# Block with adaLN, sliding-window attention and a gated MLP: w_q and later loads behind a wait for the modulation weights, a new instruction order

## The chip, the cores and the metric

The kernel runs on one core of one Trainium2 chip. The metric is device time in microseconds (us) of one execution; the number given for a kernel is the median over its timed runs. A profiled execution has its own time, and a span, which is the time from its first to its last instruction.

## What is computed

One block over a sequence of 2048 tokens of width 448 (bfloat16), cut from the reference:

```python
mod = (silu(c) @ w_mod).reshape(c.shape[0], 6, 1, -1)
sa, ca, ga, sb, cb, gb = (mod[:, i] for i in range(6))
h = layernorm(x) * (1 + ca) + sa
x = x + ga * A(h, wqkv, wo)
h = layernorm(x) * (1 + cb) + sb
x = x + gb * B(h, w_in, w_sp, b_sp, w_out)

def A(x, wqkv, wo):            # H = 16 heads of 28, window W = 256
    q, k, v = split(x @ wqkv)
    scores = q @ k.T * 28 ** -0.5
    mask = (i - j >= 0) & (i - j < W)
    return softmax(where(mask, scores, -1e9)) @ v @ wo

def B(x, w_in, w_sp, b_sp, w_out):
    z = gelu(x @ w_in)                       # 448 -> 1792
    z2 = layernorm(z[..., 896:])
    g = w_sp @ z2 + b_sp                     # mixing over the 2048 tokens
    return (z[..., :896] * g) @ w_out
```

The modulation (`mod`) is one vector of 6 x 448 numbers for all tokens. Its first two parts, sa and ca, are wanted before anything of the attention can be computed from x, since each normalized token is scaled and shifted by them.

## The kernel before

**Tiles.** The 2048 tokens are 16 tiles of 128; four tiles make a block `tb` (0 to 3). x stays in SBUF as `x_sb`. For each tile the kernel takes statistics on DVE (`bn_stats`, `bn_aggr`; function `stats`, L626 to L633), raises the variance to the power -1/2 on POOL (L633), normalizes into `xn` (`norm`, L644 on DVE or L651 on POOL) and transposes to `hT`, features on partitions. Block 0 is transposed on PE (L740) and modulated while it is copied out of PSUM (L748 to L751, on ACT or DVE). Blocks 1 to 3 are transposed by DMA, issued by SP (`turn`, L467), and modulated in place (L729 to L732).

**Attention.** `hT` times `WQK` gives Q (L797 for block 0, L763 later) and K (L821); `hT` times `wv` gives V (L841). `WQK` is a copy of the loaded `wq_st` in which each head of 28 is padded to 32 columns; function `wqk` (L615, L616) makes it in eight copies, four for K (`t_wqkk`) and four for Q (`t_wqkq`), each on ACT, DVE or POOL. Scores (L906 to L967) go to PSUM, ACT takes the exponential (L912), DVE masks (L975, L996), PE multiplies with V (L1003), DVE divides (L1017, L1019), a DMA transpose and `wo_g` follow (L1029), and DVE adds x (L1033). The second layer norm, its DMA transpose and its modulation (L1052, L1054) prepare the MLP: z from L1123 and L1144, the mixing over tokens L1168, the last product L1187, the output L1197 and L1202.

**Modulation.** The row c is turned to a column by four tiny products (`t_cT`, L514), ACT takes SiLU of it (`t_sc`, L517; it needs a table load, and the exponential later needs another). Thirty-two products with `wmodA` (`t_mA`, four groups of eight, L544) give sa and ca, which DVE copies to `modT` (`t_modA`, L573, L574). The other four parts come later from `wmodB`. While PE would have nothing to do at the start it runs products on a tile of ones (`fillers`, function `warm`, L563): 30 long and 6 short ones, whose results nobody reads.

**Loads at the start.** SP and ACT issue them, each in its own order. c (`t_c`), x in pieces (`t_x0[0]`: tiles 0 and 1; `t_x0[1]`: tiles 2 and 3; `t_x[1]`: tiles 4 to 7; `t_x[2]`, `t_x[3]`: the rest), `wmodA` in four quarters of 196 KB (`t_wmA`; 0 and 2 on SP, 1 and 3 on ACT), the K and the Q columns of wqkv in two halves each (`t_wk`, `t_wq`; half 0 on SP, half 1 on ACT), the V columns (`t_wv`, SP), and `wmodB`, 1568 KB (`t_wmB`, SP).

**The order.** Every operation is an `Op` with a number in order of its making, the engines that could run it, and the operations that it depends on (`deps`). The text `PLAN` names for each operation its engine (p PE, a ACT, d DVE, t POOL, s SP), its number and, behind points, the PSUM bank or buffer that it takes: `p42.1` is operation 42 on PE with the second choice of bank. Each engine runs its words in the order of the text and never overtakes. `Sched.waits` turns dependencies between engines into semaphore waits in front of the waiting instruction. `after` and the priorities given beside the operations served the search that wrote the text, and put no instruction into the program; `deps` do.

Numbers that the change and the prediction use: 0 `t_c`; 1, 10 `t_x0`; 2 to 5 `t_wmA`; 6, 7 `t_wk`; 8, 9 `t_wq`; 11 `t_wv`; 12 to 14 `t_x[1:]`; 15 `t_wmB`; 34 to 36 the mask on POOL; 37 `t_cT`; 38 SiLU; 39, 40 clearing `QBD`, a block-diagonal copy of Q (40 waits for `t_x[1]`); 42 to 45 `t_mA`; 46 to 81 fillers; 82, 83 `t_modA`; 100 to 103 `t_wqkk`; 104 to 107 `t_wqkq`; 108 to 111 and 116 to 119 the statistics of tiles 0, 1 and of 2, 3; 112, 184 sums of variance and epsilon (`ve_all`); 114, 115, 122, 123 `xn` of tiles 0 to 3; 125, 126, 128, 129 the modulated transposes of tiles 0, 1 and 131, 132, 134, 135 of tiles 2, 3; 136 to 149 K and Q products and evictions of tiles 0, 1; 176 to 183 the statistics of tiles 4 to 7; 185 their power; 186 and 188 to 192 their `xn`; 193 to 196 their DMA transposes; 373 the first exponential.

Of the kernel before, what the change touches and what calls it, by code (L numbers as in the profile page):

```python
# [15 lines left out]
p65.0 p78.1 d82 d125 d128 t101 p139.1 t25 t102 p56.0 d126 p81.3 p76.1 p47.0 p80.3 p59.2 p53.1 p49.2 a105 t103  # L16
d129 p140 a141 a40 p148.5 p149 a150 d116 d118 d117 d119 d176 d180 d182 d178 d177 d183 d181 d179 t104 t107
p145.6 p146 a147 p136.1 p137 a138 s11 p151.5 p152 a153 p79.2 t120 t121 d123.0 d122.1 p130.7 p133.0 a134 d41
d131 t184 t185 d186.3 p68.0 p372.0 a373.2 p142.6 p143 a144 d132 d135 p154.7 p170.1 p171 p155 p378.0 s13 d241
d247 d245 s14 d308 d242 d156 d246 s15 s193 t187 t188.1 s194 p163.0 p164 t189 t190.2 s195 t191 t192.0 s196  # L20
a379.4 p397.0 t34 t35 d248 t36 d243 d382 d312 d306 d380 d309 d374 d376 p173.6 a172 p157.1 p158 p160.7 p174
a398.1 a165 p90.0 p91 d92 a399 p404.0 d402 d310 d244 d400 d169 p161 p93.0 t85 t84 a175 a159 p86.1 p87 d88 d89
p375.0 p377 p94 a405.3 a406 p425.0 p381 p383 a197 d199 t200 d198 p210.1 p211 t249 t250 t252 t253.2 t254 d95
p217.0 p218 s16 s19 a426.0.0 p433.0 d384 d385.1 p401.0 s386 a166 d407 p403 p408 a212 p204.1 p205 d311 d219
p201.0 p202 d409 s259 t255.1 d307 d313 t314 d167 d168 s260 d251.0 t256 s258 t257.3 s261 t315 t321 t319 t99 t98
t96 t97 a434.2 p453.0 d429 d203 d436 a206 p207.1 p208 p410 d411 d209 d430 d412.2 s413 d435 a162 p427.0 p220.0
p221 a454.1.1 p461.0 p229.1 p230 d457 a428 a222 p226.0 p227 d228 p431.0 p432 a462.6 p481.0 d463 a231 a482.4.2
s852 s17 s18 p437 p438 d439 d215 d440.1 s441 p223.0 p224 a225 p232.1 d458 d216 d213 d464 p489.0 a490.2 d492
p233 p235.0 p236 a237 p459.0 p455.0 p508.0 p414.0 p415 d416 t262 t264 t263 t265 a234 p387.1 p388 d389 d486
a456 p460 p465 p466 d467 d468.0 d485 t320.1 s325 t322.2 s469 s326 s21 a214 p483.0 p272.0 p273 a509.0.0 p536.0  # L30
p269.1 p270 d491 p487.0 a484 p510.0 p488 p493 a537.5.1 p516.0 d274 d316.0 s323 t317 t318.3 p494 d390 d391 t392
t393 d512 d513 d495 d496.1 s497 d394.1 t395 s324 t330 t327 t329 a271 a511 p266.1 p267 p538.0 p275.0 p276
a517.6 d519 d518 d417 p564.0 a268 p442.1 a277 p282.0 p443 p514.0 d444 d281 p515 p283 a565.4.2 d569 p544.0 d418
d445 t419 d278 p291.1 p520 p521 d522 d446 d540 d447 d541 a539 p292 a284 p288.0 p289 t448 t449 s396 t450.0 t328
t451 s20 s848 d523.1 s524 a545.2 p572.0 d546 d547 d568 a293 p294.1 p295 a290 p238.0 p239 p542.0 p543 p548
a573.0 d574 p592.0 p549 d550 d551.0 s552 s846 a240 p470.0 p471 p566.0 a296 p285.1 p286 d472 d279 a593.3.0
p600.0 p300.0 d575 d473 d596 d280 p570.0 p301 d302 a567 p571 p576 a601.2 p619.0 d602 p577 d597 d578 d579.1
s580 a287 p525.1 p337.0 p338 d474 p526 d527 a620.4.1 p627.0 d624 d623 d603 p594.0 a339 p553.0 p554 d555 p340.1
p598.0 p341 a628.5 p647.0 d475 d630 a595 p599 p604 d556 p605 d606 d607.0 s608 s452 t476 t477 t478.2 t420 t421
t422.1 d557 t423 t479 s480 s424 t558 t559 t560 a342 p498.1 p499 p621.0 d500 p297.0 p298 a648.6.2 p675.0 d629  # L40
d651 a622 p649.0 p625.0 p331.1 p332 a299 p334.0 p626 a676.3.0 p655.0 d501 d502 t503 d333 d652 d528 d679 p631
p632 p335 d633 d336 d344 a650 p347.1 p677.0 p348 a656.4 d657 p683.0 a678 a349 p609.0 p610 d611 d658 d680
d634.2 s635 a684.5 p359.1 p360 a361 p350.0 p351 a352 d612 d343 d613 d346 d345 p703.0 a704.2.1 d707 t504 d505.0
d686 t561.1 t562 t822 t614 t615 p353.1 p354 a355 p303.0 p304 a305 p653.0 p711.0 p654 p659 p660 d661 d662.1
s663 p356.1 p705.0 p581.0 p582 a712.1 p730.0 d685 d583 d713 d708 p681.0 p682 p687 p688 d689 d690.2 d714 a706
a731.0.2 d735 d734 p732.0 a733 t821 s563 s691 s853 s847 t506 s507 d529 t530 p357 d358 p738.0 a739.5 p365.0
p709.0 p710 p715 p366 a367 p716 d717 d584 d718.1 s719 t531 t532 t533.1 d585 t586 t824 t823 t534 t587 t588
t589.2 d740 d741 p758.0 a759.1.1 d763 p760.0 p362.0 p363 a364 a761 p664.1 p665 d666 d762 p736.0 p766.0 a767.3
p737 p742 p743 d744 d745.2 s746 d667 d768 p368.0 p369 p636.1 p786.0 d769 p637 d638 a370 p764.0 p692.0 p693
d694 p765 p770 s535 s371 a787.4.2 d790 p794.0 a795.2 p771 d772 d773.0 s774 d668 d669 t670 t671 t672.0 d590  # L50
s591 d791 t673 s674 d796 d639 d797 d640 d695 d696 t697 t698 t699 p788.0 a789 p720.1 p721 d722 d723 d616.1 d617
p747.0 p792.0 p870.0 p871.1 p872 p793 p798 p799 a874 s866 p873 s618 d641 t642 d876 t700.0 t701 s702 p748 d749
# [12 lines left out]
a1050 a1051 a1053 s844 s843 s838 s865 s851 s839 s841 s869 s849 s864 s863 s859 s854 s867 s862 s837 s868 s856
d1009 d995 d1010 d1002 d1003 d970 d1004 d898 d952 d959 t820 t1011 t1012 d1013 t976 d977 t1005 d1006 p1109.0
p1115.1 d1116.1 p1118.5 p1076.3 p1112.7 p1124.4 d1119.0 t1120 p1070.5 t1117 d1113.1 t1114 t817 p1106.6 d1107.1
t1108 p1121.2 d1122.1 t1123 d1125.1 t1126 p1079.7 d1080.0 t1081 p1085.6 d1071.1 t1072 d1077.1 t1078 s857 s860
s855 s861 s858 p1142.1 p1139.7 d1086.0 p1172.6 t1087 d1143.0 d1110.1 t1111 t1144 t819 t816 p1127.3 d1140.1
t1141 p1184.0 d1185.1 t1186 p1187.4 d1188.0 t1189 p1082.2 d1083.1 t1084 p1175.1 p1181.7 d1128.0 d1176.0  # L70
p1157.0 p1130.4 d1131.2 t1177 d1158.0 p1136.5 d1137.1 p1148.1 d1149.1 t1159 t1150 d1182.1 d1173.0 t1183
p1178.3 p1190.0 d1191.1 t1192 p1154.2 d1155.1 s1129 s1138 p1088.1 t1156 d1089.1 t1090 p1133.6 t1174 p1073.1
d1074.0 t1075 p1145.2 p1097.0 p1091.1 d1092.0 p1094.4 d1179.0 t1180 d1095.3 d1146.0 p1151.5 p1197.2 p1201.1
p1202 p1100.7 p1103.3 p1198 t1147 d1152.0 t1153 s1132 d1101.2 p1160.7 s1096 s1093 d1134.0 p1166.6 d1203.1
p1193.1 p1194 s1102 s1135 d1199.0 p1205.2 p1206 d1098.3 p1163.0 d1167.2 p1169.6 s1204 d1161.1 s1099 d1195.3
s1168 d1207.2 s1200 d1104.0 s1196 d1164.3 s1162 d1170.1 s1105 s1165 s1208 s1171
# [176 lines left out]
def bass_adaLN_cond__sliding_block__mixer_gmlp__prompt_kernel(  # L253
# [159 lines left out]
    t_x0 = [load_x0(0, "sp", -98.99, 3.55)]  # L413
# [856 lines left out]
```

## Time and profile before

| what | us |
|---|---|
| timed runs, median (lowest, highest) | 279.64 (279.12, 280.51) |
| profiled run | 277.97 |
| its span | 276.2 |
| span not covered by PE's busy time of 269.2 | 7.0 |
| busy: DVE, ACT, POOL | 164.2, 124.1, 132.6 |
| PE's part of the chain that ended last | 83% |
| start of the second 16 modulation products | 7.68 |
| first exponential | 18.66 |
| last exponential ends | 109.1 |
| loads: the engines move data without a break from / to | 2 / 21 |

How to read it: PE's busy time is a modelled one, since products overlap; a PE shown as busy can still be waiting between the starts of its products. The chain follows the last instruction backward, at each step to what released it. A time "to landing" of a load counts from its issue, so it holds the time that the load stood in the queue behind others. The profiled run is one execution; the timed median lies 1.67 us above it.

### The profile page before, as it was taken

The page shows a single profiled execution, that of the slowest core. Times are in us where ns is not written, and L with a number is a line of the kernel's source. Part 1 is how long each engine was busy: PE and PEld are TensorE (multiplying, and loading weights), DVE is VectorE, ACT ScalarE, POOL GpSimd, SP SyncE. Part 2 cuts the span into 40 slices and gives each one's busy share as a digit, 9 for nine tenths or more (in the row PEclk, how much of TensorE's full clock was granted, in tenths as well). Part 3 has the DMA queues.
Part 4 walks back from the last instruction along what each step waited for, and adds up shares of the span by engine and source line. Part 5 has one row for each costly group of instructions (what it writes and reads, how often), then busy time and mean ns, then how long its engine had stood idle before and what let it go on. Part 6 is the DMA issues. An engine that isn't in the chain of part 4 may idle for free.

```text
span 276.2 us, 8438 instructions
## 1 busy us (share of the span) xinstructions
PE 269.2 (97%) x3751; PEld 155.0 (56%) x3751; DVE 164.2 (59%) x365; ACT 124.1 (45%) x146; POOL 132.6 (48%) x190
## 2 busy tenths in 40 slices
PE   7999999999999999999999999999999999999995
PEld 5976676687667766454444444444444444445452
DVE  3698999999998999968979310014302213121454
ACT  3399999998889888365885500000000000000000
POOL 7573899629185283667567003316643303241400
PEclk9999999999999999999999999999999999999999
DMA  7999548478152586768599996000000001000114
GB/s 197 267 299 188 88 80 194 89 84 133 41 60 42 44 136 148 127 115 134 108 172 188 152 220 118 0 1 0 2 0 0 17 2 33 0 0 2 33 50 133
DMA packets 67302, 25.55 MB, mean 92 GB/s; under 512 B 58497, under 2 KB 66178, under 8 KB 67266
## 3 DMA queue, kind: packets, MB, share of 16 engines
q1 hardware_dynamic: 66304, 24.21, 47.4%
q10 hardware_dynamic: 962, 0.80, 1.2%
q8 instruction: 29, 0.48, 0.8%
q14 instruction: 7, 0.06, 0.1%
HBM read 9.01 MB, written 1.84 MB: 39 GB/s over the span
## 4 chain that ended last, share of the span: by engine, by line
PE 83%; ACT 5%; DVE 4%; DMA 4%; POOL 2%; issue 1%; SPq 0%; DVEq 0%; POOLq 0%
PE ps L1168 35%; PE ps L1123 8%; PE ps L1144 8%; PE ps L1187 8%; PE ps L956 6%; PE ps L1003 5%; ACT PW L912 5%; PE ps L1029 4%; PE ps L763 4%; PE ps L821 3%; DMA hT<-xn 2%; PE ps L841 2%; DMA wmodA<-in_w_mod_dram 2%; DVE PT L975 1%; PE ps L544 1%; DVE st_all L626 1%
## 5 line engine op out<-in xcount | busy, mean ns | idle before, releaser
L1175 POOL TENSOR_TENSOR z1T<-tmpg,z1T 128x512 bf16<-128x512 bf16 x28 | 32.1, 1153 | 75.3 <-DVE tmpg L1172 75.3
L912 ACT ACTIVATE PW<-ps 128x2048 bf16<-128x2048 f32 (+1 forms) x42 | 59.8, 1450 | 7.5 <-PE ps L956 7.0
L1172 DVE TENSOR_TENSOR tmpg<-ps,bsp_bc 128x512 bf16<-128x512 f32 x28 | 19.0, 689 | 72.9 <-PE ps L1168 68.1
L1168 PE MATMUL ps<-wspB,z 128*128 128x512 bf16 x224 | 49.3, 379 | 0.0
L1168 PE MATMUL ps<-wspA,z 128*128 128x512 bf16 x224 | 49.0, 379 | 0.0
L975 DVE TENSOR_TENSOR PT<-PW,mask 128x1024 bf16<-128x1024 bf16 x56 | 41.6, 770 | 0.3
L1168 PEld LDWEIGHTS ps<-wspA,z 128*128 128x128 bf16 x224 | 21.9, 98 | 26.5 <-issue 0.4
L1168 PEld LDWEIGHTS ps<-wspB,z 128*128 128x128 bf16 x224 | 21.9, 98 | 26.3
L633 POOL TENSOR_TENSOR rs_all<-ve_all,neghalf 128x1 f32<-128x1 f32 (+2 forms) x37 | 25.1, 691 | 14.5 <-DVE ve_all L631 8.7
L1003 PE MATMUL ps<-Vaug,PT 128*128 128x32 bf16 x496 | 23.7, 177 | 0.3 <-issue 0.3
L1003 PEld LDWEIGHTS ps<-Vaug,PT 128*128 128x128 bf16 x496 | 21.5, 96 | 2.7 <-issue 0.8
L1123 PE MATMUL ps<-w_in,hT 64*128 64x448 bf16 x224 | 22.2, 349 | 0.1
L1144 PE MATMUL ps<-hT,w_in 64*128 64x512 bf16 x196 | 22.2, 376 | 0.0
L1187 PE MATMUL ps<-w_out_g,z1T 128*128 128x448 bf16 (+2 forms) x119 | 22.0, 342 | 0.0
L1197 DVE TENSOR_TENSOR fin<-ps,x_sb 128x448 bf16<-128x448 f32 (+2 forms) x17 | 9.7, 594 | 18.5 <-PE ps L1187 17.0
L626 DVE BATCH_NORM_STATS2 st_all<-x_sb 128x6 f32<-128x448 bf16 x32 | 18.9, 613 | 2.3 <-DMA x_sb<-in_A_x_dram 2.2
L1003 PE MATMUL ps<-Vaug,PW 128*128 128x32 bf16 x224 | 20.1, 176 | 0.0
L626 DVE BATCH_NORM_STATS2 st_all<-z 128x6 f32<-128x448 bf16 x32 | 18.7, 608 | 1.8 <-ACT z L1130 1.8
L651 POOL TENSOR_SCALAR xn<-x_sb,rs_all,ve_all 128x448 bf16<-128x448 bf16 x20 | 17.1, 858 | 4.8 <-DMA hT<-xn 3.5
L1152 ACT ACTIVATE z1T<-ps 128x512 bf16<-128x512 f32 x28 | 14.7, 601 | 9.2 <-PE ps L1144 9.1
L956 PEld LDWEIGHTS ps<-qT,KT 32*128 32x128 bf16 (+1 forms) x1344 | 13.5, 90 | 8.9 <-ACT PW L912 6.4
L1003 PEld LDWEIGHTS ps<-Vaug,PW 128*128 128x128 bf16 x224 | 17.6, 96 | 1.3
(103 smaller groups left out, 369.4 us busy)
## 6 DMA issues: line engine op xcount, KB each, us to landing
out_dram<-fin SPq DMA_DIRECT2D x15, 112.0 KB, 1.7
wmodB<-in_w_mod_dram SPq DMA_DIRECT2D x1, 1568.0 KB, 14.5
x_sb<-in_A_x_dram SPq DMA_DIRECT2D x3, 448.0 KB, 9.9
w_in<-in_B_w_in_dram SPq DMA_DIRECT2D x3, 448.0 KB, 5.9
w_out_g<-in_B_w_out_dram SPq DMA_DIRECT2D x1, 784.0 KB, 5.0
bsp_bc<-in_B_b_sp_dram SPq DMA_DIRECT2D x1, 512.0 KB, 5.7
x_sb<-in_A_x_dram SPq DMA_DIRECT2D x2, 224.0 KB, 4.9
hT<-xn SPq DMA_TRANSPOSE x28, 3.6
```

The lines of the kernel that those rows point to most:

```text
L626: st = [dve(0.62 if True else 0, lambda e, t=t, ci=ci, s=s: e.bn_stats(st_all[:, slot, t, ci, :], s()), deps(t), prio) for ci, s in enumer ...
L633: return pool(0.4 + 0.15 * len(tiles), lambda e: e.tensor_tensor(rs_all[:, slot, a:b], ve_all[:, slot, a:b], neghalf[:, 0:b - a], ALU.pow) ...
L912: ex = act(xdur, lambda e, out_ap=out_ap, in_ap=in_ap: e.activation(out_ap(), in_ap(), ACT.Exp, scale=SCALE), [s] + list(after), v - 8.0 + ...
L956: fm.append(lambda e, hm=hm, qi=qi, key=key, kn=kn, lo=lo, hi=hi, col=col, p0=p0, t=t, j=j: e.matmul(ps[p0:p0 + kn, hm.slot[t], col:col + ...
L975: return lock_d(0.68, lambda e: e.tensor_tensor(cols(hp.slot[0] * 2048 + 1024 * k, [[256, 4], [128, 2], [1, 128]]), cols(at_w() + pad + at ...
L1003: fns.append(lambda e, hp=hp, hO=hO, hi=hi, bi=bi, kb=kb, hd=hd, nb=nb, a=at[hi][bi], p_of=p_of: e.matmul(ps[:, hO.slot[0], 32 * hd:32 * h ...
L1123: return lambda e, kc, p0, start, stop: e.matmul(ps[:, hs[t % 2].slot[hf], 0:D], lhsT=hT[p0:p0 + 64, kc, t * 128:(t + 1) * 128], rhs=w_in[ ...
L1144: return lambda e, kc, p0, start, stop: e.matmul(ps[:, hs[b // 2].slot[b % 2], :], lhsT=w_in[p0:p0 + 64, kc, ft * 128:(ft + 1) * 128], rhs ...
L1168: m = pe(16 * MMS, [lambda e, h=h, si=si, ft=ft, tb=tb: e.matmul(ps[:, h.slot[0], :], lhsT=z2[:, si, ft * 128:(ft + 1) * 128], rhs=(wspA i ...
L1172: a = dve(0.7, lambda e, h=h, ht=ht, tb=tb: e.tensor_tensor(tmpg[:, ht.slot[0], :], ps[:, h.slot[0], :], bsp_bc[:, tb * 512:(tb + 1) * 512 ...
L1175: u = pool(1.16, lambda e, ht=ht, ft=ft, tb=tb: e.tensor_tensor(z1T[tb][:, ft, :], tmpg[:, ht.slot[0], :], z1T[tb][:, ft, :], ALU.mult), [ ...
L1187: return [lambda e, ft=ft: e.matmul(ps[:, h.slot[0], 0:hi - lo], lhsT=z1T[t // 4][:, ft, (t % 4) * 128:(t % 4 + 1) * 128], rhs=w_out_g[:, ...
```

## The change

SP's half of the w_q load gets a dependency on the last quarter of `wmodA`, `t_wmA[3]`. Since SP issues in order, all its later loads wait with it. In SP's order that load moves ahead of x tiles 2 and 3. SiLU no longer stands behind ACT's w_q load in the search's rules, but behind its w_k load; and the order of all engines is searched anew.

```diff
@@ -416,9 +416,11 @@
     t_wk = load4("d_wk", wq_st, A_wqkv, slice(D, 2 * D), slice(D, 2 * D), -98.9, (8.4, 7.9))
     t_wq = load4("d_wq", wq_st, A_wqkv, slice(0, D), slice(0, D), -98.8, (10.4, 9.3))
     t_x0.append(load_x0(1, "sp", -98.85, 9.6))
-    for row in (t_x0[:1] + t_wmA[::2] + t_wk[:1] + t_x0[1:] + t_wq[:1], [t_c] + t_wmA[1::2] + t_wk[1:] + t_wq[1:]):
+    for row in (t_x0[:1] + t_wmA[::2] + t_wk[:1] + t_wq[:1] + t_x0[1:], [t_c] + t_wmA[1::2] + t_wk[1:] + t_wq[1:]):
         for first, then in zip(row, row[1:]):
             then.after = [first]
+
+    t_wq[0].deps.add(t_wmA[3])
...
-    t_sc[0].after = t_wq[1:]
+    t_sc[0].after = t_wk[1:]
```

`PLAN` is replaced as a whole; its beginning, old and new:

```diff
-d24 d22 p50.3 p52.1 p55.0 p46.1 p57.0 p54.3 a0 a3 d23 p37.0 p71.0 p63.3 p69.1 p73.0 p74.1 p61.0 p62.3 p60.2 s1
-s2 d108 d110 s4 s6 s10 s8 s12 a5 a7 a9 a38 a39 p75.1 t27 t28 t29 t32 t33 t30 t31 a100 a106 d111 d109 t112 t113
-t26 p42.1 p43 p58.3 p48.1 p44.0 p45 d114.3 d115.1 p124.6 p77.2 p64.0 p51.3 d83 p127.0 p70.1 p66.0 p72.2 p67.3
...
+d24 d22 p50.3 p52.1 p55.0 p46.1 p57.0 p54.3 a0 a3 d23 p37.0 p71.0 p63.3 p69.1 p73.0 p74.1 p61.0 p72.1 p70.3
+p59.1 p60.2 p65.3 p51.0 p64.1 s1 s2 d108 d109 d110 d111 s4 s6 a5 s8 s10 s12 a7 a38 p42.0 p43 a39 a9 t27 t28
+t29 t32 t33 t30 t31 a101 a100 a102 d112 t113 d114.3 t34 t36 t106 t35 p49.2 p48.1 p44.1 p45 p76.0 p58.0 d115.1
...
```

Each engine's own first words, put together from the whole text:

| engine | before | after |
|---|---|---|
| SP | 1 2 4 6 10 8 12 11 13 14 15 193 to 196 | 1 2 4 6 8 10 12 11 13 14 15 193 to 196 |
| ACT | 0 3 5 7 9 38 39 100 106 105 141 40 150 147 138 153 134 373 | 0 3 5 7 38 39 9 101 100 102 125 103 150 40 141 147 138 153 131 373 |
| DVE | 108 110 111 109 114 115 83 82 125 128 126 129 116 118 117 119 176 180 182 178 177 183 181 179 123 122 41 131 186 | 108 109 110 111 112 114 115 83 82 128 129 104 105 107 126 118 119 116 117 182 180 176 183 178 181 177 179 184 123 122 41 186 134 |
| POOL | 112 113 26 101 25 102 103 104 107 120 121 184 185 187 to 192 34 35 36 | 113 34 36 106 35 120 25 121 185 187 188 26 189 to 192 |
| PE | 6 fillers, 37, 9 fillers, 42 43, 2 fillers, 44 45, 124, 3 fillers, 127 | 6 fillers, 37, 13 fillers, 42 43, 2 fillers, 44 45, 2 fillers, 127 124 |

Operations that run on another engine than before, apart from those in the table: V evictions 162, 175 and 358 (ACT to DVE), K eviction 284 (ACT to DVE), copies to `QBD` 166 (ACT to DVE) and 168, 215, 279 (DVE to ACT), modulations of `hT` 198 (DVE to POOL) and 200 (POOL to ACT), modulations for the MLP 825, 827, 832 (POOL to ACT), 828, 830 (DVE to ACT), 829, 835 (ACT to DVE), and some fifteen operations on single columns or 64 columns between DVE and POOL. SP has 112 operations in both, PE 398; ACT has 148 and 154, DVE 365 and 361, POOL 186 and 184.

More of the change, by code (lines that the diff above doesn't have):

```diff
@@ L18 @@
[L18 to L52, printed above, removed]
@@ L77 @@
+p1194 p1201.6 p1202 s1132 d1101.3 d1092.2 p1133.1 p1166.5 p1198 d1203.1 p1160.6 p1103.4 p1205.3 p1206 s1096
+d1134.0 p1163.1 s1093 d1167.2 p1169.5 s1102 d1098.3 s1135 s1204 d1161.1 d1199.0 s1099 d1195.3 s1168 d1207.2
+s1200 d1104.0 s1196 d1164.3 s1162 d1170.1 s1105 s1165 s1208 s1171
 """
```

84 lines of the change are left out of this document (58 added, 26 removed).

## The prediction

> **What bounds the kernel now.** I read four views in this order. First the chain of waits, to see which work ends last; then the timeline of the first 20 us; then the issues of the loads, a narrow window at a time, because the mean over a group hides which transfer landed when; last the busy time in stretches of 5 us, to see what a shift in the head is worth later.
>
> The chain (start, duration, what):
>
> ```profile
> 1.31 4.30 DMA wmodA<-in_w_mod_dram
> 5.75 1.72 PE ps L544 x16
> ...
> 7.89 1.49 PE ps L544 x16
> ...
> 10.30 1.05 DVE hT L751 x3
> 11.35 1.06 DVE st_all L626 x2
> ...
> 12.63 2.14 DVE st_all L626 x4
> ...
> 15.50 1.35 POOL rs_all L633
> ```
>
> The head runs from the w_mod load through the 32 modulation products (L544) and the modulated transposes (L751) to the statistics of tiles 2, 3 (x2) and 4 to 7 (x4), then POOL's power. But one link is a tie. The load of tiles 4 to 7 was issued at 3.91 us and took 8.6, the last line here (KB each, us to landing; the first is x tiles 0 and 1 into an empty queue, the second SP's later w_mod quarter, issued at about 1.8, the third SP's half of w_q, issued at 3.34):
>
> ```profile
> x_sb<-in_A_x_dram SPq DMA_DIRECT2D x1, 224.0 KB, 2.4
> wmodA<-in_w_mod_dram SPq DMA_DIRECT2D x1, 196.0 KB, 5.2
> wq_st<-in_A_wqkv_dram SPq DMA_DIRECT2D x1, 196.0 KB, 7.6
> x_sb<-in_A_x_dram SPq DMA_DIRECT2D x1, 448.0 KB, 8.6
> ```
>
> So x tiles 4 to 7 landed at 12.5 us, when DVE came free for them (12.56 below). An earlier modulation alone can't move what stands behind those statistics. The timeline of the head (start, us, engine, line):
>
> ```profile
> 5.75 1.72 PE L544 MATMUL ps<-sc_sb,wmodA 112*112 112x112 bf16 x16 [0.68 <-DMA wmodA<-in_w_mod_dram]
> 7.68 1.70 PE L544 MATMUL ps<-sc_sb,wmodA 112*112 112x112 bf16 x16
> 9.42 0.16 DVE L574 TENSOR_SCALAR modT<-ps 112x4 f32<-112x4 f32 x1 [2.85 <-PE ps L544]
> 12.56 2.21 DVE L626 BATCH_NORM_STATS2 st_all<-x_sb 128x6 f32<-128x448 bf16 x4
> 17.31 3.91 SPq L467 DMA_TRANSPOSE hT<-xn  x3
> 17.36 1.28 ACT L912 ACT_TABLE_LOAD   x1
> ```
>
> From 17 us on engines are full. In the stretches (length, then busy PE, PEld, DVE, ACT, POOL, clock, DMA share, GB/s) DVE and ACT both stand near 5 of 5; from 109 us on PE alone runs without a gap:
>
> ```profile
> 20.00:25.00 5.00, 4.87 (x83) 3.26 (x76) 4.68 (x14) 4.88 (x9) 2.73 (x6) 1.00 1.52 163
> 115.00:120.00 5.00, 5.00 (x54) 2.41 (x52) 3.51 (x12) 2.48 (x5) 4.42 (x9) 1.00 0.64 135
> ```
>
> PE has no free stretch after 109 us, so a delay or gain of the first 109 us arrives at the end whole, if the full engines between don't absorb it.
>
> **Part 1, the loads.** By issue plus landing: w_mod at 5.2, 5.6, 6.7 and 7.0 us, w_k 7.9 and 8.5, w_q 10.0 (ACT) and 10.9 (SP), x tiles 2, 3 at 10.2. The engines moved 250 to 300 KB per us from 2 us on, share 0.93 and more in every us, so the first 20 us of loads are a queue of bytes. The change makes SP's w_q half wait for ACT's second w_mod quarter (6.71), and everything SP issues is behind it: x tiles 2, 3, then 4 to 7, w_v, the rest of x, the second w_mod load, and later the transposes. The first issue (0.79) found the engines moving from 2 us, 1.2 us later; so w_q flows from about 6.8 + 1.2 = 8.0 us. What is ahead of it (x, w_mod, w_k: 1400 KB at 270 from 2.0) ends at 7.2, and ACT's half of w_q, issued after SiLU and the first clear of QBD (SiLU 4.58 to 4.75 now, 0.5 earlier without the w_q issue before it; clear 1.05; so at about 5.4), fills 0.7 more: to 7.9. The queue therefore goes dry for about 0.1 us: cost 0.1. Bounds: 0 (never dry; not below, since the bytes ahead of tiles 4 to 7 are the same) and +0.8 (ACT's half comes too late to fill it). Behind w_k now come w_q before x tiles 2, 3: that swaps 196 against 224 KB, so SP's w_q lands 0.8 earlier, at 10.1, and x tiles 2, 3 at 10.9. Tiles 4 to 7 stay at 12.5 to 12.6.
>
> **Part 2, the warming products.** Nine between the products of c and the modulation become thirteen. Six take 1.46 us and nine 2.10, so one more costs 0.213; thirteen from 2.96 end at 5.73, just as w_mod lands (5.6): cost 0, and PE's wait of 0.68 is filled. What it may bring is the clock. The 16 modulation products take 1.5 us start to start (5.75 to 7.26); at the rate of L821 later (8 take 0.61, 16 take 1.06: 0.056 for 128 columns, 0.049 for 112) 16 would take 0.8. The second 16 can't begin before 7.03, so the modulation would be in modT at about 8.1 instead of 9.4; with the slow clock it stays at 9.4. I keep both ends, and take 8.8. [...]
>
> **Part 3, DVE's queue.** Three w_q copies (WQK) come from POOL and ACT to DVE, ahead of one modulated transpose and of both groups of statistics; one transpose goes to ACT. No DVE copy of that shape is in the trace. Bounds: 0.22 (the QBD copy, 32x256) and 0.42 (sc_rep); I take 0.30, the start-to-start step of the nearest rows (xn, 128x448). Slow clock: transposes from 10.05, two of them 0.64, copies 0.9, the third 0.32, so tiles 2, 3 start at 11.9; two statistics with means, 1.3; tiles 4 to 7 start at 13.2 against 12.56: +0.65. Fast clock: two transposes from 8.75 end at 9.4, then DVE stands until w_q at 10.1, copies to 11.0, transpose, statistics from 11.3, tiles 4 to 7 at 12.9: +0.35. The sum ve_all moves to DVE (0.30 on POOL becomes 0.15), which gives back 0.15. So POOL's power, tile 4's xn and SP's four transposes (17.31 now, 1.3 us each) come 0.2 to 0.5 late. I take +0.3. POOL loses three mask operations (0.88 in all) behind xn: they run earlier, while it waits for w_q; worth 0, since SP is busy with transposes until 21.2 anyway.
>
> **Part 4, ACT's queue.** It makes all four w_k copies (0.58 each) and one transpose (0.56); from 8.5 they end at 11.4, w_k's last being at 10.3 on POOL now; the first products with all w_k start at 12.03 now, so this is covered by 0.6, and costs that if PE were ready. The second clear of QBD now stands ahead of the first K eviction and waits for x tiles 4 to 7. From there ACT needs 5.4 us (13.28 to 18.66 now) to the first exponential: 12.6 + 5.4 = 18.0 if nothing is late, 18.8 if PE's transposes of tiles 2, 3 are (DVE's delay, and one of them now stands on ACT ahead of that exponential). Between them 18.4, -0.2; I count it 0, because the modulated tiles 4 to 7, 0.3 late by part 3, are waited for next.
>
> **Part 5, the order up to 109 us.** Count by moved operations: DVE gains three V evictions (0.55), one K eviction (0.69) and one QBD copy (0.22), and loses a modulation of hT (0.56) and three QBD copies: +1.3 us on some 85 busy of 90. ACT loses 3 x 0.54, 0.59 and 0.40, gains 0.81 and 3 x 0.40: -0.6. (Three h2 modulations more on ACT, 0.81 each, fall behind 109 us, where ACT has 2.5 of 5 free: 0.) In the chain DVE carries some 5 of the 80 us from 30 to 109, ACT's exponentials 13. Bounds: -0.6 and +1.3; I take +0.3, nearer the middle.
>
> **Sum.** 0.1 + 0 + 0.3 + 0 + 0.3 = +0.7 us on a span of 276.2 (profiled run 277.97, with 1.77 around it), so 276.9 and 278.7. The three timed runs have a median of 279.64, 1.67 over that run; I put the difference on it: **280.3 us**, 0.25% up. Half a percent, 1.4 us, is about what a measurement of this kernel can tell from no change, so the forecast is "no difference that shows".
>
> **Rivals.**
>
> *A, faster: 278.0.* The head feeds ACT and PE first, not DVE. For it: ACT is as full as DVE, and "ACT PW" ends the waits of PE more often than any other in the chain. Price: first exponential at 18.0 (-0.65), ACT's load (-0.6), first K and Q products earlier by as much as w_q is early, half of 0.8 (-0.4): -1.65. Against it: tiles 4 to 7 don't land earlier, and DVE has no room for 1.3 us more. [...]
>
> *B, slower: 281.8.* DVE's queue is in order and now has w_q in it. If SP's half lands later than DVE gets there (9.4 with the fast clock, 10.7 with the slow one), all statistics stand behind it. The landing is bounded by 9.2 (issue 6.8 plus the 2.4 of an empty queue) and 14.4 (plus 7.6). At 12.0, tiles 4 to 7 start 1.3 later than in part 3: +1.95 to POOL's power, and with part 5 about +2.2. It decides from a landing of 10.7 on. Against it: the bytes ahead of it end by 8 us.
>
> *C, the wait does nothing: 279.6.* Each queue moves its bytes in order anyway, so w_mod lands when it does now, and only the swap of w_q and x remains, with parts 3 and 5 hidden. For it: w_mod's four quarters already land in order of issue.
>
> **Chances.** Forecast 0.40 (of it 0.04 faster, 0.06 slower by over half a percent), A 0.23, B 0.27, C 0.10. Faster 0.27, same 0.30 + 0.10 = 0.40, slower 0.33. The range takes A and B in with the bounds of parts 1 and 5: 277.6 to 282.4. The forecast's own is 279.1 to 281.5.
>
> **What would show it.** In the changed profile: L544 within 0.3 us of now by its first start, and the second sixteen ended by 8.1 (fast) or 9.2 (slow); SP's w_q landing near 10.1, issued near 6.8; tiles 4 to 7 landing at 12.4 to 12.9; their statistics starting at 12.9 to 13.2; first exponential 18.0 to 18.8; the transposes at 17.5 to 17.8; PE without gaps from about 109.7. I am wrong if the statistics start before 12.6 and the gapless stretch before 108.5 (A), if w_q lands after 10.7 (B), or if the stretch behind 109 us changes its length, which no step above provides for.

## The result, and the profile after

| | before | after |
|---|---|---|
| timed runs, median us (lowest, highest; runs) | 278.19 (276.91, 280.63; 20) | 280.38 (277.69, 283.97; 20) |
| profiled run, span | 277.97, 276.2 | 279.42, 277.7 |
| busy: DVE, ACT, POOL | 164.2, 124.1, 132.6 | 160.5, 128.6, 127.6 |
| w_v's load lands | 14.02 | 14.88 |
| statistics of tiles 4 to 7 start | 12.56 | 13.32 |
| first exponential starts | 18.66 | 19.02 |
| exponential 434 starts | 31.32 | 32.29 |
| last two exponentials begin | 107.23 | 109.06 |
| first product of the MLP starts | 109.17 | 111.0 |

The ratio is 1.0061 (1.0034 to 1.0089): the changed kernel is 0.6% slower. (Ratios here and below leave disturbed runs out, medians don't; it matters most for new_x_first.) The interval leaves no room for "no change". The part behind 109 us kept its length: PE runs without a gap from the first product of the MLP on, which starts at 109.17 of 276.2 before and at 111.0 of 277.7 after, so it has 167.0 and 166.7 left. All of the loss arises earlier: 0.4 us by the first exponential, 1.0 by number 434, 1.8 by the last two. (These two take 2.37 us in both kernels, so before they end at 109.6, and not at the 109.1 of the table ahead of the prediction.)

The chain of waits of the changed kernel (start, us, what):

```profile
1.77 4.76 DMA wmodA<-in_w_mod_dram
...
6.55 0.31 SPq L406
...
7.41 5.89 DMA x_sb<-in_A_x_dram
...
13.32 1.68 DVE st_all L628 x3
...
19.02 1.02 ACT PT L914
```

Before, the chain left the loads at 5.6 us and went over the modulation. Now it goes from the w_mod quarter straight to SP's waiting issue (6.55), two issues on to the load of x tiles 4 to 7, and to their statistics. The modulation isn't in it any more. The issues in narrow windows (KB, us to landing) show what SP issued behind the wait, in order:

```profile
wq_st<-in_A_wqkv_dram SPq DMA_DIRECT2D x1, 196.0 KB, 3.2
x_sb<-in_A_x_dram SPq DMA_DIRECT2D x1, 224.0 KB, 3.3
x_sb<-in_A_x_dram SPq DMA_DIRECT2D x1, 448.0 KB, 5.9
wv<-in_A_wqkv_dram SPq DMA_DIRECT2D x1, 392.0 KB, 7.0
```

Each takes less time from its issue than before (7.6, 7.4, 8.6 and 9.5 us there), but they start 3 to 4 us later: w_q lands at 9.7, x tiles 2 and 3 at 10.2, tiles 4 to 7 at 13.3, w_v at 14.9. The timeline (start, us, engine, line; in brackets the idle time before and what ended it):

```profile
8.19 0.16 DVE L576 TENSOR_SCALAR modT<-ps 112x4 f32<-112x4 f32 x1 [1.06 <-PE ps L546]
9.76 0.65 DVE L617 COPY WQK<-wq_st 112x448 bf16<-112x448 bf16 x3 [0.19 <-DMA wq_st<-in_A_wqkv_dram]
13.32 1.68 DVE L628 BATCH_NORM_STATS2 st_all<-x_sb 128x6 f32<-128x448 bf16 x3 [1.12 <-DMA x_sb<-in_A_x_dram]
14.93 0.55 PE L843 MATMUL ps<-wv,hT 112*128 112x448 bf16 x2 [0.66 <-DMA wv<-in_A_wqkv_dram]
17.65 2.61 SPq L469 DMA_TRANSPOSE hT<-xn  x2
46.97 0.23 PE L958 MATMUL ps<-qT,KT 32*32 32x32 bf16 x13 [1.06 <-issue]
```

The modulation is 1.2 us earlier than before. DVE, which came free before just as x landed (12.56 and 12.54), is now through with its three w_q copies and with tiles 2 and 3 at 12.20 and stands 1.12 us for x; PE stands 0.66 us for w_v. The last row is another matter: at 46 us PE stops for 1.06 us in the middle of one group of score products, with nothing that it waits for ("issue").

The stretch from 20 us, in the columns of the same view of before:

```profile
20.00:25.00 5.00, 4.54 (x79) 3.56 (x79) 4.41 (x11) 4.92 (x9) 1.60 (x3) 1.00 1.28 190
```

The first figure is the length. PE has fallen from 4.87 to 4.54 there and DVE from 4.68 to 4.41; ACT stays where it was (4.88 and 4.92).

### The profile page after: what moved, and what is told of

It reads as the page before. It is cut to its first block, busy times and chain, and to the rows that moved or that the text cites. A ratio compares the mean times of both kernels' runs of the same rounds, so it can differ in the third digit from the quotient of the medians.

```text
span 277.7 us, 8442 instructions
## 1 busy us (share of the span) xinstructions
PE 268.1 (97%) x3751; PEld 153.6 (55%) x3751; DVE 160.5 (58%) x361; ACT 128.6 (46%) x152; POOL 127.6 (46%) x188
## 4 chain that ended last, share of the span: by engine, by line
PE 82%; ACT 10%; DMA 4%; DVE 1%; issue 1%; ACTq 0%; SPq 0%; DVEq 0%
PE ps L1170 35%; PE ps L1125 8%; PE ps L1146 8%; PE ps L1189 8%; ACT PW L914 7%; PE ps L958 6%; PE ps L1005 5%; PE ps L823 3%; PE ps L843 3%; PE ps L1031 3%; DMA x_sb<-in_A_x_dram 2%; DMA wmodA<-in_w_mod_dram 2%; PE ps L765 2%; ACT PT L914 1%; DVE st_all L628 1%
## 5 line engine op out<-in xcount | busy, mean ns | idle before, releaser
L977 DVE TENSOR_TENSOR PT<-PW,mask 128x1024 bf16<-128x1024 bf16 x56 | 37.8, 708 | 0.7 <-ACT PW L914 0.5
L958 PE MATMUL ps<-qT,KT 32*128 32x128 bf16 (+5 forms) x1344 | 17.5, 197 | 2.5 <-issue 1.5
L823 PE MATMUL ps<-hT,WQK 112*128 112x128 bf16 x256 | 17.6, 219 | 0.7 <-ACT hT L751 0.5
L1154 ACT ACTIVATE z1T<-ps 128x512 bf16<-128x512 f32 x28 | 14.9, 601 | 7.0 <-PE ps L1146 6.9
```

Source lines behind the costliest of these rows:

```text
L823: km = lambda g, kc, start, stop, h=h, t=t: lambda e: e.matmul(ps[:, h.slot[0], g * 128:(g + 1) * 128], lhsT=WQK[0:CP, kc, 16 + 4 * g:20 + ...
L958: fm.append(lambda e, hm=hm, qi=qi, key=key, kn=kn, lo=lo, hi=hi, col=col, p0=p0, t=t, j=j: e.matmul(ps[p0:p0 + kn, hm.slot[t], col:col + ...
L977: return lock_d(0.68, lambda e: e.tensor_tensor(cols(hp.slot[0] * 2048 + 1024 * k, [[256, 4], [128, 2], [1, 128]]), cols(at_w() + pad + at ...
```

## Experiments

Four questions: is it the head or the rest; is it the wait, the load order, or both together; does the stop of PE at 46 us matter; does it pay to give evictions back to ACT. "Order before" and "new order" are the two `PLAN` texts. The ratio is always to the kernel before on the same chip (medians 278.24, 278.93 and 278.19 in the three groups below, each over 28 to 34 runs). Each kernel was profiled in one execution, so a landing or a start given below is that of one execution, while the ratios rest on all runs.

### Which part of the order, and the wait

**start_new** and **rest_new** are spliced from the two texts at exponential 434 (31 us).

```diff
 start_new:
-PLAN of the order before, up to a434
+PLAN of the new order, up to a434; t_wq[0].deps.add(t_wmA[3]); then what is left, in the order before
 rest_new:
-PLAN of the order before, behind a434
+what is left, in the new order (no wait; loads as before)
```

> The changed kernel's order (and its wait) for the words of the plan up to the first exponential of tile 2, second half (operation 434, about 31 us), the order of before for all that is left. Theory H (the head: loads that land later on some of the DMA engines, tiles 4 to 7 and the second w_mod load 0.8 to 1.2 us late, and all else follows): ratio 1.004 to 1.008, x tiles 4 to 7 landing after 13.0, exponential 434 about 1 us late. Theory O (the searched order after 31 us costs it): ratio 0.998 to 1.002, whatever the first 31 us do.

> The order of before, without the wait, up to operation 434, and the changed kernel's order for the rest. Theory H: ratio 0.998 to 1.002, tiles 4 to 7 landing at 12.5. Theory O: ratio 1.004 to 1.008, with exponentials on time at 31 us and 1.1 us or more late at 50.

Measured: start_new 279.67 us, 1.0049 (1.0014 to 1.0085); rest_new 280.84, 1.0090 (1.0062 to 1.0119). In start_new theory H held: tiles 4 to 7 landed at 13.25 and exponential 434 started at 32.36, 1.04 late. In rest_new theory O's pattern came, with more than its size: 434 on time at 31.42 and exponential 537, near 50 us, 1.95 late. The two losses sum to 1.4%, more than twice the whole, so a splice isn't a neutral cut: in rest_new PE waits for operations that the new text may expect done by then. The longest of its waits of PE from 12 to 60 us (line, releaser: us in total, times, longest):

```profile
PE ps L952 <- ACT PW L908: 1.1, 2, 0.9
```

So the head alone can carry about the whole loss; that the rest carries none is not shown by the splices.

**new_no_wait** is the changed kernel without the wait; **old_wait** is the kernel before with the wait alone, x tiles 2 and 3 still ahead of SP's w_q.

```diff
 new_no_wait:
-    t_wq[0].deps.add(t_wmA[3])
 old_wait:
+    t_wq[0].deps.add(t_wmA[3])
```

> The changed kernel without its one new dependency, so SP issues w_q, x and the rest as soon as it can; the order is the new one. If the wait is what makes the loads late (H, in its narrow form): tiles 4 to 7 land by 12.6, the second w_mod load by 23.1, ratio 1.000 to 1.003. If the order of the loads or of the engines does it (O): ratio 1.005 to 1.007, as with the wait. The modulation is in modT by 8.3 either way if the fillers alone bring the clock, and 0.3 to 1 us later if the wait does.

> The kernel before with the new dependency alone (SP's w_q behind the last quarter of w_mod; x tiles 2 and 3 still ahead of it). H, narrow: tiles 4 to 7 and the second w_mod load land 0.8 to 1.2 us later than before, ratio 1.003 to 1.006. O: no change, ratio 0.998 to 1.002, since the bytes ahead of each load are the same.

Measured: new_no_wait 278.87, 1.0007 (0.9975 to 1.0038); old_wait 278.46, 1.0017 (0.9988 to 1.0046). H in its narrow form held for the first (tiles 4 to 7 at 12.60, the second w_mod load at 23.11) and fell for the second, where O held (tiles 4 to 7 at 11.72, earlier than before). Taking the wait out repairs the changed kernel by its time, and putting it into the kernel before costs nothing that shows. So the wait costs only together with something else of the change.

The profile of new_no_wait doesn't show how the time is won. It is of an execution of 280.87 us, with a stretch of half clock from 12.68 to 16.09, and in it DVE stands for ACT's half of w_q, which now comes behind SP's loads:

```profile
11.81 0.28 DVE L616 COPY WQK<-wq_st 112x448 bf16<-112x448 bf16 x1 [1.56 <-DMA wq_st<-in_A_wqkv_dram]
```

There the statistics of tiles 4 to 7 start at 13.80 and the first exponential at 20.81, later than in the changed kernel (13.32 and 19.02).

### What else: load order, the late stop, the warming products, the evictions

```diff
 new_x_first (wait kept):
-s8 s10 s12
+s10 s8 s12
 new_win_late (first two loads of w_in):
-s413 s17 s18
+s413
...
-s396
+s396 s17 s18
 new_fill_late (four fillers behind the first K and Q products):
-p72.1 p70.3 p59.1 ... p65.3
...
+p149 p72.1 ... p140 p70.3 ... p145.4 p59.1 ... p137 p65.3
 new_evict_act (V evictions of tiles 2 and 3, a K eviction):
-d162 d175 d284
+a162 a175 a284
```

> The changed kernel with x tiles 2, 3 issued ahead of SP's w_q again, so ahead of the wait, as in the order of before. Theory Q (with the wait and w_q first the queue holds too little at 6.8 us, some engines run dry and stay behind): all 16 engines land tiles 4 to 7 by 12.2 instead of 13.3, the second w_mod load by 23.2 instead of 24.3, first scores of tile 2 about 1 us earlier, ratio 1.001 to 1.004. Rival (three slow engines are the new order's, not the queue's): tiles 4 to 7 at 13 or later, ratio 1.005 to 1.008.

Measured 279.74, 1.0012 (0.9977 to 1.0047; by the medians of all runs, 279.74 against 278.93, it is 1.003): with x tiles 2 and 3 ahead of w_q again, the wait costs nothing that shows, in the new order either. By its time theory Q held, but not by its landings: 15 of the 16 engines ended tiles 4 to 7 by 11.80 and one at 13.48, the second w_mod load came at 24.06, and w_v at 14.98, as the rival had it. This profile too is of a longer execution (281.58 us, half clock from 12.63 to 16.04), and DVE stands for w_q in it:

```profile
11.54 0.65 DVE L613 COPY WQK<-wq_st 112x448 bf16<-112x448 bf16 x3 [1.88 <-DMA wq_st<-in_A_wqkv_dram]
```

The statistics of tiles 4 to 7 start at 13.90. So in the new order the repair by either edit is shown by the times alone, and no profile shows which wait became shorter.

> The changed kernel with SP's first two w_in loads (448 KB each, issued at 41 us, wanted at 109) behind the transpose of operation 396, near 60 us. In three traces with the new order up to 31 us PE stands still for 1.0 to 1.2 us at 46 us in the middle of one group of score products, with nothing to wait for, while a 16 KB instruction block is on its way among these loads. Theory F (PE waits for instructions behind the w_in packets): the stop at 46 us is gone, 0.8 to 1.1 us less than the changed kernel, ratio 1.001 to 1.004. Rival (the stop is PE's own, or the blocks come late for another reason): still there, ratio 1.005 to 1.008.

Measured 280.64, 1.0075 (1.0042 to 1.0108). The stop at 46 us is gone in its profile, where exponential 537 starts at 49.77 (51.22 in the changed kernel, 49.70 before) and the last two at 107.27 (107.23 before); the timed runs didn't get faster, so theory F missed. One profile without the stop doesn't make a faster kernel. But this profile, of the fastest of its runs (277.66), has late loads (tiles 4 to 7 at 13.14, w_v at 15.22), and at the end of the attention nothing is left of a loss.

> The changed kernel with four of its early fillers put behind the first K and Q products (11 to 15 us). 9 of 20 runs of the changed kernel show a mean clock of 0.987 to 0.994, that is one or two stretches of 3.4 us at half clock after the first full one; 3 of 34 of before do. Theory W (four fillers fewer between 10 and 17 us let the clock fall back): at most 1 or 2 of 12 runs below 0.997, median 0.3 to 0.5 us lower than the changed kernel. Rival (the gaps that the late loads leave do it): 4 or more of 12, no change of the median. PE starts the modulation up to 0.8 us earlier in its queue, which costs nothing, as it waits for w_mod.

Measured 279.93, 1.0059 (1.0027 to 1.0091): the ratio stays. Two of its twelve runs show a lower mean clock, as theory W had it, but of the twelve of new_again (below), with all fillers early, none does, so the count decides nothing. The full clock began at 8.67 us here, at 4.87 in the changed kernel and at 4.58 in rest_new, which has the nine old fillers: it doesn't follow the number of fillers here.

> The changed kernel with the V evictions of tiles 2 and 3 and the K eviction of tile 8 back on ACT, where before has them. By part 5 of the prediction (DVE carries more of the chain than it has room for): 0.2 to 0.5 us less, ratio 1.003 to 1.005. Rival (ACT is the fuller engine up to 31 us, and the new order eased it): 0.3 to 0.8 us more, ratio 1.007 to 1.010.

Measured 284.18, 1.0188 (1.0151 to 1.0225): three evictions given back to ACT cost 1.3% over the changed kernel. Part 5's side of the bet fell, and the rival's side came with about twice its size. (Five of its six runs also have the clock's fall-back of the last section, worth some 1.1 us of the 3.6.) The longest waits of PE and of ACT from 20 to 64 us in it (line, releaser: us in total, times, longest):

```profile
PE ps L954 <- ACT PW L910: 2.2, 1, 2.2
PE ps L819 <- ACT Vaug L843: 1.1, 1, 1.1
ACT Vaug L843 <- PE ps L839: 1.7, 1, 1.7
ACT KT L831 <- PE ps L819: 1.5, 1, 1.5
```

PE waits for ACT, but ACT stands idle itself: 1.7 us in front of a returned V eviction and 1.5 us in front of the returned K eviction, until PE has made what they copy, with exponentials behind them in its order. From 20 to 25 us ACT is busy for 3.33 of 5 us (4.92 in the changed kernel). The edit put the three words at the places that DVE's had in the text, which are other places in ACT's order than before had. So the run shows what a wrong place in an order costs; it doesn't show that ACT had no room, nor what the move of the evictions is worth.

### Load order alone, and the repairs together

```diff
 old_wait_wq_first (order before):
-s10 s8 s12
+s8 s10 s12
+    t_wq[0].deps.add(t_wmA[3])
 new_x_win_fill: new_x_first, new_win_late and new_fill_late in one
 new_nw_win_fill: new_no_wait, new_win_late and new_fill_late in one
 new_again: the changed kernel, unedited
```

> The order before with the change's loads alone: the wait, and SP's w_q half ahead of x tiles 2 and 3. Theory: the late landing comes from the load order, so it shows here too: tiles 4 to 7 land at 12.8 us or later (before 12.5), their statistics follow, ratio 1.002 to 1.006. Rival: the load order costs only in an order that puts w_q copies on DVE ahead of the statistics: ratio 0.998 to 1.002, the statistics of tiles 4 to 7 no later than 12.7 us.

Measured 280.05, 1.0059 (1.0032 to 1.0085), with tiles 4 to 7 landing at 13.62. The theory held, and the rival fell: the change's two edits of the loads, put into the order before, cost all that the change costs. Its timeline shows DVE waiting for x tiles 4 to 7, 2.26 us, and PE for w_v, 1.55 us:

```profile
13.65 2.21 DVE L624 BATCH_NORM_STATS2 st_all<-x_sb 128x6 f32<-128x448 bf16 x4 [2.26 <-DMA x_sb<-in_A_x_dram]
15.50 0.93 PE L839 MATMUL ps<-wv,hT 112*128 112x448 bf16 x4 [1.55 <-DMA wv<-in_A_wqkv_dram]
```

In old_wait, with the wait alone, the same statistics start at 11.74. (The order before with w_q first and no wait was not run.)

> The changed kernel once more, on the chip of the three others. Ratio 1.004 to 1.008; PE stops for about 1 us near 46 us; two to four of the 16 DMA engines finish x tiles 4 to 7 1 us or more behind the others, and the statistics of tiles 4 to 7 start at 12.9 us or later. If the stop or the late engines are missing here at the same ratio, they weren't the cost.

Measured 279.83, 1.0043 (1.0012 to 1.0074). The ratio and the late engines are there (three of 16 end tiles 4 to 7 at 12.37 to 12.77, the middle one at 11.1); the statistics start at 12.79, a tenth earlier than expected. The stop at 46 us is missing. This doesn't clear the stop for good: the twelve runs, all at full clock, fall into two groups, five of 277.40 to 278.78 and seven of 279.81 to 280.36, and the profiled run (278.78) belongs to the lower one. The gap between them is 1.0 us, as much as the stop. Whether the upper group has the stop is not known. The chain of this second profile:

```profile
7.30 5.46 DMA x_sb<-in_A_x_dram
...
12.79 1.68 DVE st_all L628 x3
...
15.56 1.10 POOL rs_all L635
...
21.08 6.94 DMA hT<-xn
```

The load of tiles 4 to 7, their statistics, POOL's power and the DMA transposes: with a stop or without, it is the same load that the chain comes from.

> The changed kernel with three things put back or moved: x tiles 2 and 3 ahead of SP's w_q half again (the wait stays), the first two w_in loads issued only behind the transpose 396, and four of the thirteen fillers moved behind the first K and Q products. Theory: the loss is the load order behind the wait (about 1 us) and one stop of PE at 46 us (about 1 us); without both the new order is as fast as the one before or faster: ratio 0.995 to 1.002, no stop of PE near 46 us, tiles 4 to 7's statistics and the first exponential no later than 12.8 and 18.7 us. Rival: the new order itself is worse between 30 and 109 us, whatever the head does: ratio 1.004 or more, and the last exponential ends at 108.5 us or later although the stop is gone. Second rival: with this head the clock falls back more often, and mean and median then hide the gain: 1.003 to 1.008, with the runs at full clock at or below the time before.

Measured 280.30, 1.0086 (1.0057 to 1.0115). The theory failed: the repairs together are not faster than before. Its other signs missed too: the statistics start at 13.68, behind a wait of DVE for w_q of 1.37 us, and the first exponential at 21.82 (there is no stop at 46 us). The second rival failed, since the seven runs with the full clock have a mean of 280.17. The first rival's number was met, and its sign: the last exponentials begin at 110.80.

> The changed kernel without the wait (w_q still ahead of x tiles 2 and 3 on SP), with the late w_in loads and the four late fillers. Theory as for the kernel before this one: what the wait cost and what the stop of PE cost are both gone, ratio 0.994 to 1.002, no stop near 46 us. Rival (the order of the work from 30 to 109 us is worse): 1.004 or more. If this one is at 1.00 and the one with x first and the wait is not, it is the wait that costs; the other way round it is w_q ahead of x.

Measured 280.60, 1.0102 (1.0060 to 1.0144): a miss again, and the rival's number. Its profile has no stop at 46 us, but three others, of 0.50 us at 68.91, of 0.70 at 104.17 and the longest:

```profile
96.34 0.19 PE L1000 MATMUL ps<-Vaug,PT 128*128 128x32 bf16 x1 [1.38 <-issue]
```

That is 2.6 us, and late: exponential 712 starts at 91.07 (91.70 in the changed kernel), the last two at 110.00 (109.06). Late w_in loads and late fillers, which changed nothing that shows each by itself, cost 0.7 to 0.9% together where the loads are repaired. Why was not found, and a loss of the new order between 30 and 109 us, which both rivals name, is not excluded.

### The DMA queue in all of them

The busy share of the DMA engines from 9 to 11 us, in the one profile of each, separates the kernels with both edits of the loads from the others:

| kernel | wait | w_q first | head | share, 9 to 11 us | tiles 4 to 7 land | w_v lands | ratio |
|---|---|---|---|---|---|---|---|
| before | no | no | before | 1.13 | 12.54 | 14.02 | 1 |
| rest_new | no | no | before | 1.12 | 12.05 | 13.67 | 1.0090 |
| old_wait | yes | no | before | 1.11 | 11.72 | 13.10 | 1.0017 |
| new_x_first | yes | no | new | 1.12 | 13.48 | 14.98 | 1.0012 |
| new_x_win_fill | yes | no | new | 1.08 | 13.12 | 14.51 | 1.0086 |
| new_no_wait | no | yes | new | 1.11 | 12.60 | 14.21 | 1.0007 |
| new_nw_win_fill | no | yes | new | 1.11 | 12.63 | 14.29 | 1.0102 |
| after | yes | yes | new | 0.95 | 13.30 | 14.88 | 1.0061 |
| new_again | yes | yes | new | 1.00 | 12.77 | 14.29 | 1.0043 |
| start_new | yes | yes | new | 0.92 | 13.25 | 15.04 | 1.0049 |
| new_win_late | yes | yes | new | 0.90 | 13.14 | 15.22 | 1.0075 |
| new_fill_late | yes | yes | new | 1.02 | 12.39 | 14.47 | 1.0059 |
| new_evict_act | yes | yes | new | 1.05 | 12.80 | 14.24 | 1.0188 |
| old_wait_wq_first | yes | yes | before | 0.82 | 13.62 | 15.45 | 1.0059 |

The rows that the share is read from, in stretches of 2 us (busy PE, PEld, DVE, ACT, POOL, clock, DMA share, GB/s). Before:

```profile
7.00:9.00 2.00, 2.00 (x22) 1.94 (x22) 0.00 (x0) 0.45 (x1) 0.49 (x1) 1.00 1.12 275
9.00:11.00 2.00, 2.00 (x26) 1.78 (x25) 1.33 (x6) 0.74 (x3) 1.33 (x5) 1.00 1.13 265
```

After:

```profile
7.00:9.00 2.00, 1.88 (x30) 1.84 (x31) 0.64 (x4) 0.71 (x2) 0.05 (x1) 1.00 1.09 258
9.00:11.00 2.00, 1.49 (x19) 1.08 (x17) 1.77 (x7) 1.72 (x4) 0.75 (x2) 1.00 0.95 261
```

old_wait, with the wait but x first:

```profile
7.00:9.00 2.00, 2.00 (x31) 1.79 (x29) 1.14 (x6) 0.45 (x1) 0.48 (x1) 1.00 1.13 276
9.00:11.00 2.00, 1.86 (x26) 1.66 (x25) 1.94 (x6) 1.28 (x3) 2.00 (x6) 1.00 1.11 314
```

old_wait_wq_first:

```profile
7.00:9.00 2.00, 2.00 (x33) 1.94 (x32) 0.81 (x4) 0.48 (x2) 0.52 (x2) 1.00 0.98 257
9.00:11.00 2.00, 2.00 (x28) 1.75 (x26) 1.86 (x5) 1.02 (x3) 2.00 (x6) 1.00 0.82 190
```

With one of the two edits or none the share is 1.08 to 1.13 (above 1 the times of the packets add up to more than the stretch on 16 engines, so some of them overlap). With both edits it is 0.82 to 1.05, although SP has issued tiles 4 to 7 and w_v by 8.6 us, so part of the 16 engines seem to stand while others still work. A lower share is not always fewer bytes: from 7 to 11 us the changed kernel moved 258 and 261 GB/s against 275 and 265 before, 42 KB less in all, and new_again (255 and 290) no less than before. In the order before the loss is plain: 190 GB/s against 314 with the wait alone. Either edit alone leaves the share at 1.08 to 1.12: x tiles 2 and 3 issued ahead of the wait are bytes to move meanwhile, and without the wait SP has issued everything down to w_v by 5.8 us. The landing of tiles 4 to 7 is that of the last of the 16 engines, which differs more between executions of one program (13.30 and 12.77 in after and new_again, the middle engine 11.36 and 11.1); in new_x_first 15 engines were done at 11.80 and one at 13.48.

The table doesn't tie the time to the landing. new_fill_late has tiles 4 to 7 earlier than before and is 0.6% slower, new_x_first has them later than the changed kernel and is not, and three kernels with a share of 1.08 to 1.12 are slower by 0.9 to 1.0%.

## Why the prediction came out as it did

**Time right, sign right, size short.** The forecast was 0.25% up on the kernel before; 0.61% was measured (1.7 us of 278.2; 1.5 us between the two profiled spans, where +0.7 was forecast). "No difference that shows" did not come true: the interval excludes no change, and 0.61% lies just on the side "slower by over half a percent", which had 0.33. That 280.3 lies so near 280.38 is partly luck: it was built on a median of 279.64 for the kernel before, which over 20 runs was 278.19, and the base too high by 1.45 made up for the difference too small.

**Part 1 has the step that failed: "Tiles 4 to 7 stay at 12.5 to 12.6".** They landed at 13.30, and at 12.77 in new_again. The two landings ahead came as worked out or better: SP's w_q at 9.74 (10.1 forecast), x tiles 2 and 3 at 10.16 (10.9). The sum looked for a dry queue at 8 us; the busy share falls from 9 to 11. The size of "cost 0.1" depends on the measure. By the share from 7 to 11 us (1.02 after, 1.12 before, 0.90 in old_wait_wq_first) it is 4 x 0.10 / 1.12 = 0.36 us and 4 x 0.22 / 1.12 = 0.79 us of queue; by the bytes moved it is 42 KB, 0.16 us, in the changed kernel, nothing in new_again, and 186 KB, 0.7 us, in old_wait_wq_first. All lie inside the bounds of 0 to 0.8. What the sum didn't have is that a load has landed when the last of 16 engines is done: three of them ended tiles 4 to 7 at 13.02 to 13.30, where the middle one was done at 11.36, earlier than the middle one before (11.75). The sum treated the 16 engines as one pipe. In whole kernels the pair of edits costs about 0.4%, some 1.2 us, where the forecast had 0.1 us: 1.0059 less 1.0017 in the order before, 1.0061 or 1.0043 less 1.0007 or 1.0012 in the new one (each ratio to about 0.003). That the late engines make this loss fits the profiles of the order before; in the new order it is not shown.

**Part 2: the fast case came true** (modT at 8.19, and 7.78 in new_again; 8.1 forecast). But the kernel before is as fast in other executions: with the wait alone, in its own order, it has modT at 7.74. The four more products aren't needed for it: full clock began at 4.58 us in rest_new with nine and at 7.34 in new_win_late with thirteen. That more of them bring the full clock sooner was the author's assumption, and no run shows it. The start differs between executions of one program (4.87 in after, 4.34 in new_again), and over all profiles that record it, it lies between 4.3 and 9.5 us (9.49 in before). The earlier modulation brought nothing that shows, as the ties in the head said: the loads are next in line.

**Part 3: right time, other cause.** Statistics of tiles 4 to 7 at 13.32 and 12.79 (12.9 to 13.2 forecast), the power 0.59 late (16.09, before 15.50), SP's transposes 0.34 late (17.65, +0.3 forecast). It was to be DVE's queue, but DVE was free at 12.20, earlier than before; it waited 0.19 us for w_q and 1.12 for x. The three copies took 0.65 us where 0.9 was taken. The sum of the fast case has a slip besides: statistics of tiles 2 and 3 from 11.3 and 1.3 us for them give 12.6, not 12.9, so in the case that came true DVE's queue would have cost nothing by the prediction's own terms.

**Part 4: counted as nothing, and nothing it was** to the accuracy of one execution: first exponential at 19.02 and 18.48 (18.0 to 18.8 forecast), before 18.66.

**Part 5: +0.3 can't be told from nothing.** At equal loads the new order costs nothing that shows: 1.0061 and 1.0043 against 1.0059 with both edits, 1.0012 against 1.0017 with the wait alone; but 0.003 of a ratio is 0.8 us. One operation was counted the wrong way round, there and in the list of moved operations: V eviction 358 goes from DVE to ACT, so DVE gains two V evictions and gives one away. With it the count is +0.2 us for DVE, not +1.3, and +0.5 for ACT, not -0.6. new_evict_act was to price the move and doesn't, since ACT stood idle in front of the returned evictions.

**The rivals.** A (faster) fell: the statistics start at 13.32, not before 12.6, and the first product of the MLP at 111.0, 1.8 us later than before. B (slower) forecast the measured side with the wrong load: in the changed kernel w_q was at DVE in time, 9.74 against the 10.7 from which it decides; it was x tiles 4 to 7, and w_v on PE, that came late. Its wait of DVE for w_q is real, though: it shows in the new order where one of the two edits is taken out (1.56 and 1.88 us). C (the wait does nothing) holds for the wait alone, as old_wait shows, but not with w_q ahead.

**What stays open.** How the loads are dealt to the 16 engines when SP issues four of them within 2 us is not in the trace, so why some of them end late is not shown, only that they do. How much of the 1.2 us comes from the late loads isn't shown either: new_fill_late had tiles 4 to 7 at 12.39 and was no faster, and new_win_late had them at 13.14 in an execution as fast as before. The stop of PE near 47 us, about 1 us in some executions, stays a rival for part of the loss in the new order; the order before shows none in its three profiles, and there the two edits cost as much. And the kernels with all repairs are slower than those with one.

## What to carry to other kernels

A wait put into a queue of loads should leave enough bytes issued ahead of it to last until the first load behind it flows (with both edits the share of 9 to 11 us was 0.82 to 1.05 here, with one 1.08 to 1.12); look at the busy share of the DMA engines after the release, and at the last engine's landing, not at the bytes in total. Test two edits of a load order apart and together: here the wait alone (in either order) and w_q first alone (in the new one) cost nothing that shows, and the pair 0.4%. When an operation is given to another engine, look at its place in that engine's order too: the engine stands there until the operation's input is ready, with all that comes behind (1.7 and 1.5 us of ACT in new_evict_act). And before a profile is set beside a timed result, see whether the profiled execution is a typical one: those of the two repaired kernels were 2 us slower than their medians.

## What the runs showed of the hardware

**PE stopped where the profile shows nothing that held it.** Stops of 1.0 to 1.3 us near 46 to 48 us are in six profiles and missing in eight, even of the same program (after and new_again). The traces show blocks of 16 KB on the queue marked "instruction" (q8) every 4 to 6 us there. In after one started at 44.63, 6.2 us behind the one before it, and took 1.02; PE stopped from 45.91 to 46.97. In before one started at 42.50, 4.5 us behind the one before it, and PE didn't stop. But in after the blocks at 57.92, 83.66 and 93.09 come 5.4 to 6.0 us behind the ones before them too, and PE has no such stop there. So what stops PE is not shown.

**The clock fell back in five profiles.** In new_no_wait, new_x_first, new_x_win_fill, new_evict_act and old_wait_wq_first PE runs one stretch of 3.41 us at half clock after the first full one. The clock (third figure from the right) in new_x_win_fill, where it was full from 7.03 to 13.86 and half to 17.27:

```profile
10.45:13.86 3.41, 1.67 (x24) 1.36 (x24) 2.47 (x9) 1.46 (x4) 0.81 (x3) 1.00 1.10 276
14.00:17.00 3.00, 2.82 (x25) 2.70 (x26) 2.97 (x12) 1.67 (x3) 1.63 (x4) 0.50 1.12 324
18.00:20.00 2.00, 2.00 (x25) 1.57 (x22) 0.00 (x0) 1.58 (x4) 0.00 (x0) 1.00 1.03 251
```

PE was busy for 1.67 of the 3.41 us just before. In all five the clock had been full for some time (6.83 us in three, 10.24, 54.61), and in the last 3.41 us before the fall PE was busy for 1.25 to 1.67. In before and after, which show no such stretch up to 275.7 us and to the end, PE was busy for at least 3.02 and 2.35 us of each 3.41 from the start of the full clock on. What sets a fall off is not shown.

Nine of 20 timed runs of the changed kernel show such a loss by their granted clock (0.99 in place of 1.00), and none of 12 of new_again; they were 1.1 us longer in the mean (281.1 against 280.0), so this isn't what makes the changed kernel slower: its runs at full clock alone have means of 279.98 and 279.38, those of before 278.2 to 278.5.
